# Row numbers of a group written behind its gates, and clearings tied to score tiles, in a one-core attention and mixture-of-experts kernel

## The chip, the core and the metric

The kernel runs on one core of one Trainium2 chip. The metric is the device time of one execution in microseconds. Two timed runs of the kernel before gave 2300.16 and 2305.29 us, median 2302.72 us. One more execution was profiled; it took 2296.34 us. Lines such as L443 are lines of the kernel before, unless the text says that they are of the changed kernel. PE is the matmul engine, DVE the vector engine, ACT the scalar engine, POOL the GpSimd engine, SP the engine that only issues transfers here.

## The reference

The inputs are u and v of shape 8 x 2496 x 256 and z of shape 8 x 2496 x 64, in float32, with an expert layer of 8 experts (256 to 1024 to 256).

```python
scores = (1 / S) * z @ z.T                    # per batch, S = 2496
out = (np.maximum(scores, 0) ** 2) @ v
x = (u * out).reshape(B * S, D)               # 19968 tokens of 256
logits = normalised(x) @ normalised(expert_emb).T / tau
expert_idx = argmax(logits, axis=1)           # one expert a token
gate = softmax(logits)[expert_idx]
out[token] = gate * (np.maximum(x @ w1[e], 0) @ w2[e])
```

The products are made from pairs of 16-bit halves (a value's rounded half and what is left of it), three products for one.

## The kernel before, in words

**Stage one, attention and routing.** The scores are symmetric, so a batch's 20 key tiles of 128 rows stand against five groups of up to 512 queries (the last has 448), and a score tile that lies above the diagonal is made once and reached again by a transposing DMA. There are 8 batches x 5 groups = 40 groups, and for each of them a loop over 20 key tiles. A step of this loop (the loop over `steps` at the end of the function) has three kinds of work:

- `scores` (L255 to L265): two matmuls into `sc`, then ACT makes relu and the square in `a`; three tiles ahead of their use.
- `parts` (L267 to L296): DVE splits `a` into two 16-bit halves, a cast (L284) and a subtraction (L285), in `hl` or in `joint`; `state["dv"]` is always the latest of these casts. SP issues the transposing DMA.
- `values` (L313 to L327): six matmuls of the halves with the halves of v, into two accumulators `acc` (L323, L325, L327).

PE follows the order of the program as it is written. DVE, ACT and POOL follow an order that a scheduler makes from the program by its own estimate of when things are ready; an engine then runs its list strictly in that order, and an instruction that waits holds up everything behind it. `tc.issue_after(ins)` adds an edge for this order alone: what is written under it comes behind `ins` on its own engine, without a semaphore.

**Routing.** When a group's 20 steps are over, `route` (L342 to L493) returns a list of pieces, and one of them runs behind the `values` of each later step. `gate_x` (L360) multiplies both accumulators with u into `xt`, which has one buffer (L362, two instructions). `turn` (L365) turns `xt` on PE (L368, L369), two steps later at the first; ACT copies the result and sums its squares (L379, L375). `root` (L618 to L632) and `scale` make scales on DVE, `splits` (L405, L406) write each token's x as two 16-bit halves into `row`, `top` and `exps` choose the expert, `gates` (L436 to L443) writes two more columns of `row`: the gate (L441) and the token's number (L443), `rank` and `place` find the row of the buffer `xs` that each token goes to (`dsti`, L467), and `scatters` issues four indirect DMAs from POOL, which carry `row` to `xs` (L473).

`row` has two buffers that the groups use in turn (`rows[par]`). What a group writes into its buffer may not overwrite what the scatter of the group before the last one still reads. The token numbers (L443) depend on nothing but this: they are made of the constant `idb` and the number of the group.

**Other work of stage one.** DVE also searches the next batch's z and v for their greatest values (L117, from loads `scan` with two buffers), splits z (L188, L189) and v (L233), and converts the experts' weights (L514 to L566). Of the last, short v tile half of the low part is cleared (L230); in a batch's last, short group the last 64 columns of `xt` are cleared (L349). POOL issues the plain loads of all this, in the same list as the scatters.

**Stage two, the experts.** From about 1445 us on, 8 experts' tokens are read from `xs` in tiles of 256 or 128, with matmuls at L881 to L883 and L905 to L907, and scattered to the output (L912).

Of the kernel before, what the change touches and what calls it, by code (L numbers as in the profile page):

```python
# [14 lines left out]
ALU = mybir.AluOpType  # L15
# [4 lines left out]
P = 128  # L20
# [11 lines left out]
def ceil_div(a, b):  # L32
    return -(-a // b)
# [11 lines left out]
def relu2_attention_then_moe(ctx, tc, zT, uT, v, emb, tau, w1, w2, ident, tri, iota_e, out):  # L45
    nc = tc.nc
    B, D, S = uT.shape
# [170 lines left out]
    def v_split(b, s):  # L218
        vt = vraw.pop((b, s))
        vv = vring.tile([P, 2 * D], F16, name="vv", tag="vv")  # L220
        k = scan[b, "cv"]
        if s == NST - 1:

            lo, hi = slice(0, DQ), slice(DQ, P)
            vh = wk.tile([P, D], F16, name="vh", tag="vh", bufs=1)
            nc.scalar.activation(vv[lo, 0:D], vt[lo], AF.Copy, scale=k[lo])
            nc.vector.tensor_copy(vv[lo, D:], vv[lo, 0:D])
            nc.scalar.activation(vh[hi], vt[hi], AF.Copy, scale=k[hi])
            nc.vector.scalar_tensor_tensor(vv[hi, 0:D], vt[hi], k[hi], vh[hi], op0=ALU.mult, op1=ALU.subtract)
            nc.vector.memset(vv[hi, D:], 0.0)  # L230
        else:
            nc.scalar.activation(vv[:, 0:D], vt, AF.Copy, scale=k)
            nc.vector.scalar_tensor_tensor(vv[:, D:], vt, k, vv[:, 0:D], op0=ALU.mult, op1=ALU.subtract)  # L233
        Vs[b, s] = vv

    state = {"pm": False}
# [105 lines left out]
    def route(b, g, acc, ut):  # L342

        t0, n = groups[g]
        nj = ceil_div(n, P)
        eps, oinv = scan[b, "out"]
        xt = rt.tile([P, 2, 512], F32, name="xt", tag="xt", bufs=1)
        if n < nj * P:
            nc.vector.memset(xt[:, :, n:nj * P], 0.0)  # L349
        x = rt.tile([P, 4, 2 * XH], F32, name="x", tag="x", bufs=1)  # L350
        xk = x.rearrange("p j (k c) -> p j k c", k=2)[:, :, :, 0:P]
        par = (b * NG + g) % 2
# [2 lines left out]
        row = rows[par]  # L355
        rowi = row.bitcast(I32)
        row16 = row.bitcast(F16)
        loc = {}
# [77 lines left out]
        def gates():  # L436
            sm = rt.tile([P, 4], F32, name="sm", tag="sm")
            nc.vector.tensor_reduce(sm[:, :nj], loc["ex"][:, :nj, :], axis=AX.X, op=ALU.add)
            nc.vector.tensor_scalar_add(sm[:, :nj], sm[:, :nj], 1e-9)
            nc.vector.reciprocal(sm[:, :nj], sm[:, :nj])  # L440
            nc.vector.scalar_tensor_tensor(row[:, :nj, D:D + 1], sm[:, :nj].unsqueeze(2), oinv,  # L441
                                           loc["dn"][:, :nj].unsqueeze(2), op0=ALU.mult, op1=ALU.mult)
            nc.vector.tensor_scalar_add(rowi[:, :nj, D + 1:D + 2], idb[:, :nj].unsqueeze(2), float(b * S + t0))  # L443

        def rank():
            ob = loc["ob"].rearrange("p j e -> p (j e)")
# [44 lines left out]
        def sq(j):  # L491
# [3 lines left out]
        return [gate_x, lambda: None, turn(0), both(turn(1), take(0)), both(take(1), sq(0)), both(turn(2), sq(1)),  # L495
                both(turn(3), take(2)), both(take(3), sq(2)), sq(3), root, scale, top, exps, splits(0),
                splits(2), gates, rank, place, scatters]


# [472 lines left out]
    for i, (b, g, q, s) in enumerate(steps):  # L972
# [16 lines left out]
        if i == 6:  # L989
# [7 lines left out]
            idb = iot[:, 4 * E:4 * E + 4]  # L997
# [23 lines left out]
        if b == 0 and g == 0:  # L1021
            v_split(b, s)
        if b + 1 < B:
            if (g == NG - 2 and q >= NST - early) or (NG > 1 and g == NG - 1) or NG == 1:
                k = q - (NST - early) if g == NG - 2 else q + early
                if k < NST:
                    v_split(b + 1, k)
                    if k + VAHEAD < NST:
                        v_load(b + 1, k + VAHEAD)
            if g == max(0, NG - 2) and q == 0:  # L1030
                for k in range(min(VAHEAD, NST)):
                    v_load(b + 1, k)
            while todo and todo[0][0] <= i - b * NB and not (todo[0][1] and state["pm"]):
                with tc.issue_after(state["at"]), tc.issue_after(state["dv"]):
                    todo.pop(0)[2]()
# [11 lines left out]
        if q == NST - 1:  # L1047
            while queue:
                queue.pop(0)()
            queue = route(b, g, accs.pop((b, g)), uts.pop((b, g)))  # L1050
            if b == B - 2 and g == NG - 1 and KA:
                queue.append(table_a)
            queue.pop(0)()
# [100 lines left out]
```

## Time and profile before

| what | value |
|---|---|
| timed runs, median | 2302.72 us (2300.16 to 2305.29) |
| profiled execution, own time | 2296.34 us |
| its span, first to last instruction | 2294.6 us |
| mean granted PE clock over the span | 0.984 |
| PE busy | 2166.9 us, 94% |
| DVE busy | 1373.0 us, 60% |
| ACT busy | 1062.1 us, 46% |
| POOL busy | 538.4 us, 23% |

How to read it: "busy" is an engine's time inside instructions. A matmul's end is modelled, so that 512 columns show 0.38 us while the next one starts 0.216 us later. A row of a table of waits gives the waiting engine and line, what it waited for, the total in us, the number of waits and the longest. In a timeline, what stands in brackets is the engine's idle time ahead of the instruction and what ended it. In a table by windows each row has a stretch of the span, its length, each engine's busy time with the number of its instructions, the granted PE clock, the mean busy share of the DMA engines, and GB/s.

### The profile page before, as it was taken

The page shows a single profiled execution, that of the slowest core. Times are in us where ns is not written, and L with a number is a line of the kernel's source. Part 1 is how long each engine was busy: PE and PEld are TensorE (multiplying, and loading weights), DVE is VectorE, ACT ScalarE, POOL GpSimd, SP SyncE. Part 2 cuts the span into 40 slices and gives each one's busy share as a digit, 9 for nine tenths or more (in the row PEclk, how much of TensorE's full clock was granted, in tenths as well). Part 3 has the DMA queues.
Part 4 walks back from the last instruction along what each step waited for, and adds up shares of the span by engine and source line. Part 5 has one row for each costly group of instructions (what it writes and reads, how often), then busy time and mean ns, then how long its engine had stood idle before and what let it go on. Part 6 is the DMA issues. An engine that isn't in the chain of part 4 may idle for free. (4 is left out here: it accounts for less than half of the span.)

```text
span 2294.6 us, 41344 instructions
## 1 busy us (share of the span) xinstructions
PE 2166.9 (94%) x14634; PEld 1416.5 (62%) x14634; DVE 1373.0 (60%) x4067; ACT 1062.1 (46%) x2193; POOL 538.4 (23%) x695
## 2 busy tenths in 40 slices
PE   6898999989999989999899999999999999999999
PEld 2444444444444444444444444788888888888898
DVE  7777767767778777687777855633333333333333
ACT  7566557656756656566666654222222222222221
POOL 1214124133134124224213201121212121212121
PEclk9999999999999999999999999999999999999999
DMA  7847766783974975776665573442333333237675
GB/s 190 197 98 194 149 161 164 142 211 99 173 195 116 203 152 146 162 163 183 133 153 132 118 166 78 126 119 66 75 84 75 84 93 66 50 82 205 141 194 129
DMA packets 518035, 313.84 MB, mean 137 GB/s; under 512 B 473845, under 2 KB 479230, under 8 KB 509632
## 3 DMA queue, kind: packets, MB, share of 16 engines
q1 hardware_dynamic: 474400, 165.55, 36.7%
q0 software_dynamic: 43136, 145.22, 21.0%
q8 instruction: 117, 1.92, 0.4%
q14 instruction: 94, 0.77, 0.1%
q10 hardware_dynamic: 288, 0.39, 0.1%
HBM read 277.53 MB, written 59.60 MB: 147 GB/s over the span
## 5 line engine op out<-in xcount | busy, mean ns | idle before, releaser
L263 ACT ACTIVATE a<-sc 128x512 f32<-128x512 f32 (+1 forms) x480 | 269.7, 562 | 193.1 <-PE sc L261 119.9
L912 POOL DMA_INDIRECT out_dram<-ot,me x159 | 154.6, 972 | 675.4 <-DVE ot L911 643.2
L264 ACT ACTIVATE a<-a 128x512 f32<-128x512 f32 (+1 forms) x480 | 286.8, 598 | 13.1
L473 POOL DMA_INDIRECT xs<-row,dsti x160 | 169.3, 1058 | 470.9 <-DVE joint L284 169.0
L327 PEld LDWEIGHTS <-vv 128*128 128x128 f16 x1600 | 158.3, 99 | 189.2 <-issue 14.8
L325 PEld LDWEIGHTS <-vv 128*128 128x128 f16 x1520 | 150.3, 99 | 185.7 <-issue 37.0
L323 PEld LDWEIGHTS <-vv 128*128 128x128 f16 x1600 | 158.0, 99 | 164.5 <-issue 7.6
L907 PE MATMUL po<-w,hl 128*128 128x256 f16 x928 | 253.0, 273 | 0.0
L906 PE MATMUL po<-w,hh 128*128 128x256 f16 x928 | 253.0, 273 | 0.0
L905 PE MATMUL po<-w,hh 128*128 128x256 f16 x928 | 253.0, 273 | 0.0
L323 PE MATMUL acc<-tt,vv 128*128 128x512 f16 (+1 forms) x640 | 242.2, 378 | 0.0
L325 PE MATMUL acc<-tt,vv 128*128 128x512 f16 (+1 forms) x640 | 242.0, 378 | 0.0
L911 DVE TENSOR_SCALAR ot<-po,me,w 128x256 f32<-128x256 f32 x116 | 58.3, 541 | 220.3 <-PE po L907 220.3
L327 PE MATMUL acc<-tt,vv 128*128 128x512 f16 (+1 forms) x640 | 188.7, 377 | 0.0
L260 PE MATMUL sc<-z 128*128 128x512 f16 (+1 forms) x480 | 176.4, 367 | 5.9 <-DVE z L189 3.1
L261 PE MATMUL sc<-z,z 128*128 128x512 f16 (+1 forms) x480 | 176.3, 367 | 0.0
L379 ACT COPY x<-pt 128x264 f32<-128x264 f32 x160 | 59.7, 373 | 172.4 <-PE pt L369 170.0
L906 PEld LDWEIGHTS <-hh 128*128 128x128 f16 x1272 | 124.4, 98 | 15.3 <-issue 1.0
L907 PEld LDWEIGHTS <-hl 128*128 128x128 f16 x1272 | 124.4, 98 | 14.4
L905 PEld LDWEIGHTS <-hh 128*128 128x128 f16 x1272 | 124.4, 98 | 14.2
L368 PE MATMUL pt<-rhs,xt 128*128 128x136 f32 x320 | 69.2, 299 | 44.2 <-DVE xt L362 43.0
L368 PEld LDWEIGHTS pt<-rhs,xt 128*128 128x128 f32 x320 | 60.8, 200 | 77.2 <-DVE xt L362 54.3
(3890 smaller groups left out, 5266.5 us busy)
## 6 DMA issues: line engine op xcount, KB each, us to landing
w<-wsd SPq DMA_DIRECT2D x64, 1026.0 KB
wa<-wsd SPq DMA_DIRECT2D x46, 1024.0 KB
w<-wsd SPq DMA_DIRECT2D x42, 1024.0 KB
wb<-wsd SPq DMA_DIRECT2D x24, 1026.0 KB
vt<-in_v_dram POOLq DMA_DIRECT2D x140, 128.0 KB, 2.8
scan<-in_v_dram POOLq DMA_DIRECT2D x56, 320.0 KB, 4.1
wr<-in_w_dram POOLq DMA_DIRECT2D x16, 1024.0 KB, 7.1
wsd<-wo POOLq DMA_DIRECT2D x16, 1024.0 KB, 5.2
```

The lines of the kernel that those rows point to most:

```text
L260: nc.tensor.matmul(sc[:, :n], z1[:, ss], z1[:, t0:t0 + n], start=True, stop=False)
L261: nc.tensor.matmul(sc[:, :n], z1[:, ss], z2[:, t0:t0 + n], start=False, stop=True)
L263: state["at"] = nc.scalar.activation(a[:, :n], sc[:, :n], AF.Relu, scale=2.0 ** -SHIFT).ins
L264: nc.scalar.activation(a[:, :n], a[:, :n], AF.Square)
L323: nc.tensor.matmul(o, va, ph, start=first, stop=False)
L325: nc.tensor.matmul(o, vb, ph, start=False, stop=False)
L327: nc.tensor.matmul(o, vb if last else va, pl, start=False, stop=ends)
L473: put = nc.gpsimd.indirect_dma_start(xs[:, :], bass.IndirectOffsetOnAxis(ap=loc["dsti"][:m, j:j + 1], axis=0), row[:m, j, :], None)
L905: nc.tensor.matmul(o, hh[:, f, t], wh, start=(f == 0), stop=False)
L906: nc.tensor.matmul(o, hh[:, f, t], wl, start=False, stop=False)
L907: nc.tensor.matmul(o, hl[:, f, t], wh, start=False, stop=(f == NF - 1))
L912: put = nc.gpsimd.indirect_dma_start(out, bass.IndirectOffsetOnAxis(ap=me.bitcast(U32)[:, j, 1:2], axis=0), ot[:, j, :], None, bounds_chec ...
```

## The change

Three instructions of DVE are tied to a place in the order. The token numbers come behind the gates of the same group. Both clearings come behind the score tile's cast that was the latest when they were written in the program. Nothing is added, left out or changed in size.

```diff
@@ v_split, the last key tile
             nc.vector.scalar_tensor_tensor(vv[hi, 0:D], vt[hi], k[hi], vh[hi], op0=ALU.mult, op1=ALU.subtract)
-            nc.vector.memset(vv[hi, D:], 0.0)
+            with tc.issue_after(state["dv"]):
+                nc.vector.memset(vv[hi, D:], 0.0)
@@ route
         if n < nj * P:
-            nc.vector.memset(xt[:, :, n:nj * P], 0.0)
+            with tc.issue_after(state["dv"]):
+                nc.vector.memset(xt[:, :, n:nj * P], 0.0)
@@ route, gates
-            nc.vector.scalar_tensor_tensor(row[:, :nj, D:D + 1], sm[:, :nj].unsqueeze(2), oinv,
-                                           loc["dn"][:, :nj].unsqueeze(2), op0=ALU.mult, op1=ALU.mult)
-            nc.vector.tensor_scalar_add(rowi[:, :nj, D + 1:D + 2], idb[:, :nj].unsqueeze(2), float(b * S + t0))
+            gw = nc.vector.scalar_tensor_tensor(row[:, :nj, D:D + 1], sm[:, :nj].unsqueeze(2), oinv,
+                                                loc["dn"][:, :nj].unsqueeze(2), op0=ALU.mult, op1=ALU.mult).ins
+            with tc.issue_after(gw):
+                nc.vector.tensor_scalar_add(rowi[:, :nj, D + 1:D + 2], idb[:, :nj].unsqueeze(2), float(b * S + t0))
```

The added lines shift the numbers: the cast L284 is L285 in the changed kernel, the subtraction L285 is L286, `xt` L362 is L364, the gate L441 is L443, and the token numbers L443 are L446.

The lists of PE, ACT and SP are the same in both kernels. On POOL, at two places (one in the second batch, one in the sixth), the load of u and one of three scan loads change places. On DVE the rows move as follows.

Before, DVE at the end of the second batch's first group: `hl` and `joint` are halves of score tiles, `mx` the search in an expert's weights, `xt` the product that PE turns, `row_99` the buffer of the group after it.

```order
L284 CAST hl__2747<-a 128x4x128
L285 TENSOR_TENSOR hl__2747<-a,hl__2747 128x4x128
L443 TENSOR_SCALAR row_99<-iot 128x4
L284 CAST hl__2769<-a 128x4x128
L514 TENSOR_REDUCE mx<-wr_2473 128x1
L285 TENSOR_TENSOR hl__2769<-a,hl__2769 128x4x128
L514 TENSOR_REDUCE mx<-wr_2473 128x1
L362 TENSOR_TENSOR xt<-acc_2341,ut 128x512
```

The same place in the changed kernel:

```order
L285 CAST hl__2747<-a 128x4x128
L286 TENSOR_TENSOR hl__2747<-a,hl__2747 128x4x128
L285 CAST hl__2769<-a 128x4x128
L517 TENSOR_REDUCE mx<-wr_2473 128x1
L286 TENSOR_TENSOR hl__2769<-a,hl__2769 128x4x128
L517 TENSOR_REDUCE mx<-wr_2473 128x1
L364 TENSOR_TENSOR xt<-acc_2341,ut 128x512
```

The token numbers are gone from this place; those of each group now stand next to its gate, or one row behind it.

Before, DVE at the seam of the first two batches, some rows behind the routing of the first batch's fourth group: `dsti` are the scatter's rows, `wo` converted weights.

```order
L467 TENSOR_REDUCE dsti<-pos 128x4
L284 CAST hl__2289<-a 128x448
L566 SCALAR_TENSOR_TENSOR wo<-wr_825,wup,wo 128x512
L285 TENSOR_TENSOR hl__2289<-a,hl__2289 128x448
L566 SCALAR_TENSOR_TENSOR wo<-wr_825,wup,wo 128x512
L284 CAST hl__2310<-a 128x4x128
L285 TENSOR_TENSOR hl__2310<-a,hl__2310 128x4x128
L443 TENSOR_SCALAR row_100<-iot 128x4
L284 CAST hl__2331<-a 128x4x128
```

The same place in the changed kernel:

```order
L470 TENSOR_REDUCE dsti<-pos 128x4
L285 CAST hl__2289<-a 128x448
L569 SCALAR_TENSOR_TENSOR wo<-wr_825,wup,wo 128x512
L286 TENSOR_TENSOR hl__2289<-a,hl__2289 128x448
L569 SCALAR_TENSOR_TENSOR wo<-wr_825,wup,wo 128x512
L285 CAST hl__2310<-a 128x4x128
L351 MEMSET xt 128x2x64
L286 TENSOR_TENSOR hl__2310<-a,hl__2310 128x4x128
L285 CAST hl__2331<-a 128x4x128
```

The token numbers are gone and the clearing of `xt`, which stood some rows earlier before, has come in.

A third place, at the end of the second group of the second batch and again of the sixth: before, DVE, with `wm`, `wmb` and `dg` from the scales of the weights and `smxv` the search in v.

```order
L285 TENSOR_TENSOR hl__3203<-a,hl__3203 128x4x128
L527 TENSOR_SCALAR wmb<-wm 2x1
L362 TENSOR_TENSOR xt<-acc_2773,ut 128x512
L529 TENSOR_SCALAR dg<-idt,wmb 2x2
L362 TENSOR_TENSOR xt<-acc_2774,ut 128x512
L117 TENSOR_REDUCE smxv<-scan 128x1 x2
```

In the changed kernel:

```order
L530 TENSOR_SCALAR wmb<-wm 2x1
L117 TENSOR_REDUCE smxv<-scan 128x1
L532 TENSOR_SCALAR dg<-idt,wmb 2x2
L364 TENSOR_TENSOR xt<-acc_2773,ut 128x512
L364 TENSOR_TENSOR xt<-acc_2774,ut 128x512
L286 TENSOR_TENSOR hl__3203<-a,hl__3203 128x4x128
L117 TENSOR_REDUCE smxv<-scan 128x1
```

One of the two searches now stands ahead of both products, and the subtraction behind them.

## The prediction

> **What bounds the kernel now.** I read the table by windows first, to see which stage the change can touch.
>
> ```profile
> core 0: us, PE busy (x) PEld busy (x) DVE busy (x) ACT busy (x) POOL busy (x), PEclk, DMA share, GB/s
> 100.00:1430.00 1330.00, 1232.95 (x6118) 616.29 (x6117) 973.07 (x3217) 796.85 (x1717) 358.19 (x495) 0.98 0.66 153
> 1445.00:2295.00 850.00, 842.09 (x8093) 756.67 (x8090) 315.86 (x592) 194.48 (x333) 162.69 (x167) 1.00 0.43 107
> ```
>
> Stage two is PE, 842 of 850 us at full clock, and the change moves nothing in it. In stage one PE is the fullest engine too, but it stands still for 97 of 1330 us and its clock is not full; DVE is busy for 973 us, 73%. So stage one ends when PE does, and I look for what holds PE. The table of DVE's waits has as its largest rows of stage one:
>
> ```profile
> DVE row L443 <- DMA xs<-row,dsti: 99.3, 24, 5.5
> DVE xn2c L618 <- ACT sq L375: 59.5, 15, 8.7
> DVE smxv L117 <- DMA scan<-in_v_dram: 42.9, 20, 5.3
> ```
>
> The first row is the token numbers: 24 of the 40 wait for the scatter that last read their buffer, 99.3 us, 4.1 us each. DVE is not the fullest engine, so this costs only what PE then lacks. PE's table of waits, the rows that matter here:
>
> ```profile
> PE pt L368 <- DVE xt L362: 43.0, 17, 5.5
> PE pm L449 <- DVE ob L427: 15.6, 6, 3.6
> PE pm L141 <- DVE wm L524: 4.4, 2, 2.6
> PE acc L323 <- DVE hl__10565 L284: 2.7, 1, 2.7
> PE acc L323 <- DVE hl__14653 L284: 0.6, 1, 0.6
> ```
>
> The timeline ties the two. This is one of the 24 places: POOL's last scatter of a group, DVE, then PE.
>
> ```profile
> 245.44 0.90 POOL L473 DMA_INDIRECT xs<-row,dsti  x1 [0.30 <-issue]
> ...
> 243.37 0.69 DVE L285 TENSOR_TENSOR hl__2747<-a,hl__2747 128x512 f16<-128x512 f32 x1
> 248.01 0.17 DVE L443 TENSOR_SCALAR row<-iot 128x4 int32<-128x4 f32 x1 [3.95 <-DMA xs<-row,dsti]
> 248.11 0.43 DVE L284 CAST hl__2769<-a 128x512 f16<-128x512 f32 x1
> ...
> 250.24 1.28 DVE L362 TENSOR_TENSOR xt<-acc,ut 128x512 f32<-128x512 f32 x2
> ...
> 245.25 0.59 PE L327 MATMUL acc<-joint,vv 128*128 128x512 f16 x2
> ...
> 247.84 0.59 PE L327 MATMUL acc<-tt,vv 128*128 128x512 f16 x2
> ```
>
> DVE is free at 244.06, stands for 3.95 us until a scatter has landed, and everything behind the token numbers starts late: a cast, a subtraction, two searches in a weight, and the product `xt`. PE ends the group's accumulators at 245.84, has 2.6 us of other work ahead of the turn (to 248.43) and then waits:
>
> ```profile
> 250.98 0.50 PE L368 MATMUL pt<-rhs,xt 128*128 128x136 f32 x2 [2.54 <-DVE xt L362]
> ```
>
> I went through the 24 places like this, one by one: each is followed within 4 us by a wait of PE. The first and the last, DVE and PE:
>
> ```profile
> 142.34 0.17 DVE L443 TENSOR_SCALAR row<-iot 128x4 int32<-128x4 f32 x1 [3.88 <-DMA xs<-row,dsti]
> 143.10 0.27 PE L141 MATMUL pm<-smbv,ones_f 1*128 1x1 f32 x1 [2.59 <-DVE wm L524]
> ...
> 1425.40 0.17 DVE L443 TENSOR_SCALAR row<-iot 128x4 int32<-128x4 f32 x1 [3.22 <-DMA xs<-row,dsti]
> 1427.06 0.38 PE L368 MATMUL pt<-rhs,xt 128*128 128x136 f32 x1 [1.25 <-DVE xt L362]
> ```
>
> In 15 places PE waits for `xt`, in 7 for a cast (`hl`, at the seams of batches), in 2 for `wm`.
>
> **The change part by part.** *Token numbers behind the gates.* The instruction itself, 0.17 us, is neither added nor taken away; its wait goes. By then the buffer must be free anyway, because the row splits of the same group stand ahead of the gates and write it first; the wait for the scatter falls to them. The smallest room over all groups is the last one's: its token numbers were let go at 1425.40 (above), its first split runs here:
>
> ```profile
> 1463.16 0.35 DVE L405 TENSOR_SCALAR row<-x,up 128x256 f16<-128x256 f32 x1
> ```
>
> That is 38 us after the landing, so the moved wait finds its scatter done. I price it at nothing.
>
> What PE gets back, by the rows above. Of the 43.0 us for `xt`, two waits belong to a late scan load, not to the token numbers:
>
> ```profile
> 106.59 0.82 DVE L117 TENSOR_REDUCE smxv<-scan 128x1 f32<-128x640 f32 x1 [5.35 <-DMA scan<-in_v_dram]
> 108.07 0.59 PE L368 MATMUL pt<-rhs,xt 128*128 128x136 f32 x1 [5.48 <-DVE xt L362]
> ...
> 822.91 0.82 DVE L117 TENSOR_REDUCE smxv<-scan 128x1 f32<-128x640 f32 x1 [2.56 <-DMA scan<-in_v_dram]
> 824.39 0.38 PE L368 MATMUL pt<-rhs,xt 128*128 128x136 f32 x1 [4.48 <-DVE xt L362]
> ```
>
> So `xt` gives 43.0 - 5.5 - 4.5 = 33.0 us in 15 waits. The seven casts run from 2.7 us (`hl__10565`) to 0.6 us (`hl__14653`), 12.9 us together. `wm` gives 4.4 us. Sum: 50.3 us. That is half of DVE's 99.3 us; the other half was PE's cushion, as in the place shown, where DVE would have come to `xt` (2.1 us behind the token numbers) at about 246.2 us, just behind the accumulators, and with 1.3 us for the two products the turn would have found them at 247.5 us.
>
> *The clock.* Right after the place shown the windows say:
>
> ```profile
> 251.60:255.00 3.40, 3.40 (x10) 1.86 (x11) 2.14 (x4) 0.89 (x3) 0.75 (x1) 0.50 0.49 139
> ...
> 1360.90:1364.30 3.40, 3.40 (x11) 1.86 (x11) 0.76 (x2) 0.89 (x3) 0.75 (x1) 0.50 0.71 146
> ```
>
> For 3.4 us the granted clock is 0.50 and PE gets 10 or 11 matmuls done; with a full clock it is 19:
>
> ```profile
> 255.00:258.40 3.40, 3.40 (x19) 1.00 0.47 93
> ```
>
> Eleven of the 24 places are followed by such a stretch (these are the first and the last); each costs half of 3.4 us, 1.7 us, together 18.7 us. If the wait of PE brings them on, they go with it. The Trainium skill ("TensorE: Matmul & The Clock Gate", section "HAM oscillation — how this bites in real kernels") gives the rule as no idle gaps of PE over some 3.4 us; by it, waits of 0.6 to 3.2 us would not lower the clock and this term would be nothing. The trace speaks against the rule as a threshold: the half clock begins 0.6 us behind a gap of 2.54 us.
>
> *Clearings.* 16 instructions of 0.165 us, now inside a cast and subtraction:
>
> ```profile
> L349 DVE MEMSET xt<- x8: 165/165/165, 187.3 to 1434.2; 128x128 f32 x8
> L230 DVE MEMSET vv<- x8: 165/165/165, 60.4 to 1273.1; 64x128 uint32 x8
> ```
>
> 2.6 us at most over the kernel, on an engine with 27% idle time: nothing. Without that cover it would be the 2.6 us.
>
> *The search ahead of `xt`.* At two places one search in v now stands ahead of the products. The second of these before:
>
> ```profile
> 1003.07 0.67 DVE L362 TENSOR_TENSOR xt<-acc,ut 128x512 f32<-128x512 f32 x1
> ...
> 1003.80 0.67 DVE L362 TENSOR_TENSOR xt<-acc,ut 128x512 f32<-128x512 f32 x1
> 1004.68 0.82 DVE L117 TENSOR_REDUCE smxv<-scan 128x1 f32<-128x640 f32 x1 [0.21 <-DMA scan<-in_v_dram]
> ```
>
> It waited until 1004.68 for its load; ahead of `xt` (there at 1003.07) it would take 0.8 us and wait up to 1.7 us. PE had no wait at these two turns, so some of it is absorbed: between 0 and 2 x 2.5 us, with two clock stretches 8.4 us. I take 2, nearer the lower end.
>
> *What comes back.* With the token numbers gone something else is last. The 25 turns that had no such wait show how much: 10.0 us for late scan loads, 0.4 us each. For the 15 freed turns that makes 6 us, and I add 1 us, some half of a stretch at half clock: 7 us back. The lower bound is nothing, the upper one half of the sum (below). A faster stage one raises the DMA share only from 0.66 to about 0.69, so I add nothing for contention.
>
> **Sum:** 50.3 + 18.7 - 2 - 7 = 60 us off the profiled execution's own 2296.3 us, 2236.3 us. That execution lies 6.4 us under the median of the timed runs, 2302.72 us; I add half of this and predict **2239 us**.
>
> **The rivals.**
>
> *Another wait takes the place.* Scan loads and the squares of ACT also hold DVE (42.9 and 59.5 us), and the six waits for `ob` (15.6 us, at each seam, where DVE itself is late) stay. If these take half of the 69 us back, the time is 2296.3 - 34.5 + 3 = 2265 us. For it: the scan chain has two buffers, and two of the 25 free turns show it. Against it: 23 of 25 do not.
>
> *The clock does not follow.* If the stretches at half clock have other causes, 18.7 us stay: 2258 us. For it: the mean of 0.98 over 1330 us is 27 us, some 16 stretches, so five have no token numbers ahead of them, and 13 of the 24 waits have no stretch behind. Against it: eleven stand right behind a wait. It is what the Trainium skill's rule above would give.
>
> *The wait was hidden.* If PE's waits for `xt` were due to the accumulators being late and not to DVE's list, nothing moves: 2299 us. Against it: the accumulators of the place shown were done 4 us ahead of `xt`.
>
> *Slower.* The wait for the scatter moves to the row splits. If scatters land later than those start, all 38 groups with a predecessor wait there, on the path that leads to the gates, at 4.1 us each and PE's half of it: 38 x 4.1 x 0.51 = 79 us, and 38 x 11 / 24 x 1.7 = 30 us of clock, against 69 us saved: 2296.3 + 40 + 3 = 2339 us. It decides from the point at which scatters slip by 38 us or more. Against it: they have landed 2.6 us after the last issue in the place shown.
>
> **How the numbers follow.** Forecast 0.72, another wait 0.14, the clock 0.06, hidden 0.05, slower 0.03. The range goes down to 2216 us (all 69 us and 11 of the 15.6 us for `ob`, should DVE reach the seams earlier) and up to 2272 us, past the first two rivals; what lies beyond is hidden, slower, and tails. A measurement of this kernel tells about 2% from no change, that is 2256.7 us here. Faster by more: nearly all of the forecast and small parts of two rivals, 0.77. Within 2%: the rest of those and hidden, 0.20. Slower: 0.03.
>
> **What would show it.** Right: the row of DVE waiting for `xs<-row,dsti` is gone and no such wait stands at the splits; PE's wait for `xt` falls from 43 us to some 16; the seven waits for casts at the seams are gone; stretches at half clock in stage one fall from 16 to five or six; stage two keeps its 850 us. Wrong: a wait for scatters at the splits, DVE's idle time come back as waits for `scan`, or a full set of half-clock stretches without the waits.

## The result, and the profile after

The changed kernel took 2222.5 us (median of 2219.11 and 2225.89), against 2302.72 us before: a ratio of 0.9652, with a 95% interval of 0.957 to 0.973. Timed again with seven executions of the changed kernel and eleven of the kernel before, the ratio was 0.9637, interval 0.961 to 0.966 (the last run below). The forecast was 2239 us in a range of 2216 to 2272 us: the right way, inside the range, the gain 80 us where 64 were forecast.

The profiled execution took 2219.11 us, its span 2217.2 us. First the table by windows, with the two stages cut where they now lie:

```profile
100.00:1353.00 1253.00, 1208.85 (x6118) 609.74 (x6117) 973.91 (x3215) 795.66 (x1717) 359.73 (x494) 0.99 0.70 162
1368.00:2217.00 849.00, 841.60 (x8088) 756.40 (x8083) 316.15 (x594) 194.10 (x333) 162.82 (x167) 1.00 0.43 107
```

The 6118 matmuls that took 1330 us of stage one before take 1253 us; stage two is as long as it was. In the table of DVE's waits neither the token numbers nor the splits wait for `xs<-row,dsti` any more (one wait of `xt`, 0.4 us, is put down to it); its largest rows of stage one are those that stood second and third before:

```profile
DVE xn2c L621 <- ACT sq L377: 68.4, 18, 8.4
DVE smxv L117 <- DMA scan<-in_v_dram: 40.3, 15, 5.4
```

PE's waits, the rows that answer to those shown of before:

```profile
PE pm L452 <- DVE ob L429: 15.5, 6, 3.7
PE pt L370 <- DVE xt L364: 10.7, 3, 5.4
```

The wait for `xt` fell from 43.0 us in 17 to 10.7 us in 3, the two behind late scan loads and a small one. The seven waits for casts and the two for `wm` that the prediction counted are gone; other casts still hold PE, for up to 2.2 us each. The place that the prediction took as its example, DVE and PE:

```profile
235.00 0.69 DVE L286 TENSOR_TENSOR hl__2747<-a,hl__2747 128x512 f16<-128x512 f32 x1
235.77 0.43 DVE L285 CAST hl__2769<-a 128x512 f16<-128x512 f32 x1
...
237.91 1.28 DVE L364 TENSOR_TENSOR xt<-acc,ut 128x512 f32<-128x512 f32 x2
...
239.46 0.59 PE L328 MATMUL acc<-tt,vv 128*128 128x512 f16 x2
239.89 0.40 PE L370 MATMUL pt<-rhs,xt 128*128 128x136 f32 x2
240.12 0.40 PE L371 MATMUL pt<-rhs,xt 128*128 128x136 f32 x2
```

Between the subtraction and the next cast DVE now stands for 0.08 us instead of 4 us, and PE goes from `values` to the turn without a bracket. The token numbers wait for nothing where they are now, and neither does the first split, to which the wait for the scatter fell; the views of these two lines name no idle time ahead of them:

```profile
L446 DVE TENSOR_SCALAR row<-iot x40: 161/165/168, 93.1 to 1392.7; 128x4 int32<-128x4 f32 x40
```

```profile
L407 DVE TENSOR_SCALAR row<-x,up x160: 310/348/523, 77.8 to 1388.8; 128x256 f16<-128x256 f32 x160
```

**Where the 77 us came from.** PE issues the same 14,634 matmuls in the same order in both kernels, so the two traces can be laid over each other, matmul by matmul, and the difference of each step from one start to the next sorted: PE's waits of over 0.15 us, what else differs in steps that touch a stretch at half clock, and the rest. The other two columns do the same with the profiled executions of two runs below: the token numbers tied alone, and the changed kernel once more.

| us saved against the profiled execution of before | changed kernel | token numbers alone | changed kernel, once more |
|---|---|---|---|
| waits of PE over 0.15 us | 50.7 | 49.4 | 42.7 |
| steps that touch a stretch at half clock | 16.4 | 14.9 | 5.2 |
| the rest (in the first column nearly all inside the turns, L368 and L369) | 10.1 | 9.2 | 11.5 |
| sum, from the first matmul to the last | 77.2 | 73.5 | 59.4 |

The last column is the slowest of the seven executions, 2236.6 us, and it shows how much the parts vary: two executions of one kernel differ by 8.0 us in waits elsewhere and 11.2 us at half clock. The 24 matmuls of PE that waited behind the token numbers don't vary: they waited for 50.5 us before and for none in all three columns.

### The profile page after: what moved, and what is told of

Its sections match the earlier page's. It is cut to its first block, busy times and chain, and to the rows that moved or that the text cites. A ratio compares the mean times of both kernels' runs of the same rounds, so it can differ in the third digit from the quotient of the medians.

```text
span 2217.2 us, 41314 instructions
## 1 busy us (share of the span) xinstructions
PE 2141.7 (97%) x14634; PEld 1409.6 (64%) x14634; DVE 1374.8 (62%) x4067; ACT 1060.1 (48%) x2193; POOL 540.5 (24%) x695
## 4 chain that ended last, share of the span: by engine, by line
PE 70%; DVE 10%; DMA 7%; issue 6%; ACT 4%; POOL 3%; SPq 0%; POOLq 0%; DVEq 0%; ACTq 0%
PE acc L328 9%; PE acc L324 9%; PE acc L326 8%; PE po L908 6%; PE po L910 6%; PE po L909 6%; PE sc L261 3%; PE sc L262 3%; POOL xs L476 2%; DMA wsd<-wo 2%; DMA scan<-in_v_dram 1%; PE pt L371 1%; PE pt L370 1%; ACT a L265 1%; ACT a L264 1%
## 5 line engine op out<-in xcount | busy, mean ns | idle before, releaser
L324 PE MATMUL acc<-tt,vv 128*128 128x512 f16 (+1 forms) x640 | 236.9, 370 | 0.0
L326 PE MATMUL acc<-tt,vv 128*128 128x512 f16 (+1 forms) x640 | 236.8, 370 | 0.0
L328 PE MATMUL acc<-tt,vv 128*128 128x512 f16 (+1 forms) x640 | 184.3, 370 | 0.0
L195 POOL DMA_DIRECT2D vt<-in_v_dram x140 | 76.2, 546 | 82.4 <-DVE vv L234 40.2
L908 PE MATMUL po<-wb,hh 128*128 128x256 f16 x344 | 93.8, 273 | 1.0 <-DMA wb<-wsd 1.0
```

The lines of the kernel that those rows point to most:

```text
L324: nc.tensor.matmul(o, va, ph, start=first, stop=False)
L326: nc.tensor.matmul(o, vb, ph, start=False, stop=False)
L328: nc.tensor.matmul(o, vb if last else va, pl, start=False, stop=ends)
L908: nc.tensor.matmul(o, hh[:, f, t], wh, start=(f == 0), stop=False)
```

## The experiments

Times are medians; each ratio is against the kernel before, run beside it on the same chip (its medians there were 2297 to 2310 us).

**Which part of the change.** The first run ties the token numbers alone (`...` stands for lines left out):

```diff
             nc.vector.memset(vv[hi, D:], 0.0)
...
             nc.vector.memset(xt[:, :, n:nj * P], 0.0)
...
+            with tc.issue_after(gw):
+                nc.vector.tensor_scalar_add(rowi[:, :nj, D + 1:D + 2], idb[:, :nj].unsqueeze(2), float(b * S + t0))
```

> The token numbers are tied behind their gates, both clearings stay where the kernel before has them. Theory (the wait of the token numbers is all): about 2223 us, the changed kernel's time within 0.5%, no wait of DVE for scatters, PE's wait for xt some 11 us. Rival (the clearings inside score tiles, or the reordering as a whole, give part of it): over 2240 us.

Measured: 2219.3 us, ratio 0.961 (0.9575 to 0.964); PE's wait for `xt` 10.8 us in 3. The second ties the clearings alone:

```diff
+            with tc.issue_after(state["dv"]):
+                nc.vector.memset(vv[hi, D:], 0.0)
...
+            with tc.issue_after(state["dv"]):
+                nc.vector.memset(xt[:, :, n:nj * P], 0.0)
...
             nc.vector.tensor_scalar_add(rowi[:, :nj, D + 1:D + 2], idb[:, :nj].unsqueeze(2), float(b * S + t0))
```

> Both clearings are tied, the token numbers stay untied. Theory: 2303 us within 0.5%, DVE still waits some 99 us for scatters in 24 places. Rival (the clearings give part of it): under 2285 us.

Measured: 2307.3 us, ratio 0.9985 (0.997 to 1.000), with DVE's wait as in the kernel before:

```profile
DVE row L445 <- DMA xs<-row,dsti: 99.8, 24, 6.3
```

The token numbers are the whole of it; the clearings are worth nothing that can be measured.

**The dose.** Token numbers of every other group:

```diff
-            nc.vector.tensor_scalar_add(rowi[:, :nj, D + 1:D + 2], idb[:, :nj].unsqueeze(2), float(b * S + t0))
+            with (tc.issue_after(gw) if par else nullcontext()):
+                nc.vector.tensor_scalar_add(rowi[:, :nj, D + 1:D + 2], idb[:, :nj].unsqueeze(2), float(b * S + t0))
```

> Only the token numbers of every other group (the 20 groups with the second row buffer) are tied; the clearings stay as before. Of the 24 places 13 are in these groups, with 27.1 of the 50.5 us of PE's waits and 6 of the 11 stretches at half clock. Theory (each place is paid by itself): about 0.54 of the gain, 2260 us, between 2250 and 2270; 11 waits of DVE for scatters are left, some 45 us. Rival (a place removed is paid at the next one, DVE or PE catch up): under a quarter of the gain, over 2283 us. Rival (one kind of place carries it all): near 2223 or near 2303 us.

Measured: 2264.2 us, ratio 0.9795 (0.976 to 0.983), 46 us below the 2310.0 us of the kernel before beside it, where the full change's ratio makes 84 us: 0.55 of it (by the ratio's interval, 0.46 to 0.67). DVE's and PE's waits:

```profile
DVE row L444 <- DMA xs<-row,dsti: 46.5, 11, 5.5
...
PE pt L368 <- DVE xt L362: 28.4, 11, 5.7
```

13 of the 24 waits went, and with them the share of the gain that their own PE waits had foretold (0.54). Of the 50.5 us at the 24 matmuls of PE, 24.9 us are left. So these places are paid one by one, and what is saved at one is not lost at the next.

**The wait without the token numbers.** The changed kernel, with an instruction added that has the same wait, since it writes into the same buffer, and whose numbers nothing uses:

```diff
             with tc.issue_after(gw):
                 nc.vector.tensor_scalar_add(rowi[:, :nj, D + 1:D + 2], idb[:, :nj].unsqueeze(2), float(b * S + t0))
+            nc.vector.tensor_scalar_add(rowi[:, :nj, D + 2:D + 3], idb[:, :nj].unsqueeze(2), float(b * S + t0))
```

> The changed kernel, with one more instruction for each group that writes the same numbers into a column of the row buffer that nothing reads, and is not tied. It brings the wait for the scatter back without moving the token numbers or the clearings; it adds 40 x 0.17 us to DVE. Theory (the wait in the middle of DVE's list is the cost): about 2303 us, 24 waits, some 99 us, half-clock stretches back to some 16. Rival (the token numbers next to their gates, or the order of the other rows, make the gain): 2223 to 2230 us.

Measured: 2303.0 us, ratio 0.998 (0.996 to 1.000): the whole gain is lost again.

```profile
DVE row L447 <- DMA xs<-row,dsti: 99.1, 24, 6.6
...
PE pt L370 <- DVE xt L364: 44.9, 18, 6.1
```

At 22 of the same 24 matmuls PE waits again, for 49.1 us where it was 50.5. The token numbers themselves are where the change puts them, as are the clearings. So it is not their nearness to the gates that helps, but that nothing in the middle of DVE's list waits for a scatter.

**Would another buffer have done?** To make room for a third row buffer, both runs have a shorter ring for v; the first is the control.

```diff
-    vring = actx.enter_context(tc.tile_pool(name="vring", bufs=NST + 5))
+    vring = actx.enter_context(tc.tile_pool(name="vring", bufs=NST + 1))
```

> The kernel before with a ring of 21 instead of 25 buffers for the halves of v, only to make room for the next run, its control. No theory rests on its time; expected 2300 to 2320 us with the same 24 waits for scatters.

The second, against the control:

```diff
-    rows = [cst.tile([P, 4, ROW], F32, name=f"row{i}") for i in range(2)]
+    rows = [cst.tile([P, 4, ROW], F32, name=f"row{i}") for i in range(3)]
...
-        row = rows[par]
+        row = rows[(b * NG + g) % 3]
```

> The control, with three row buffers instead of two and the token numbers untied. Theory (the scheduler lists an instruction that waits for nothing but a buffer at the moment at which it takes the buffer to be free, whichever buffer that is, and that moment is too early on the chip): the token numbers stand at the same places of DVE's list, one group further ahead, and the 24 waits, some 97 us, and the time of the control stay within 0.7%. Rival (two buffers are too few): the waits go and the time falls by about 75 us under the control's.

Measured: control 2315.7 us, ratio 1.009 (1.006 to 1.012); three buffers 2313.7 us, ratio 1.007 (1.004 to 1.009), 0.1% apart. The waits, control and then three buffers:

```profile
DVE row L443 <- DMA xs<-row,dsti: 83.7, 24, 6.1
```

```profile
DVE row L443 <- DMA xs<-row,dsti: 76.0, 22, 6.4
```

A third buffer does not cure it: the scheduler lists the token numbers a group earlier, at the same places. In the control's trace a group's token numbers stand behind the scatters of the group two before; with three buffers they stand behind those of the group three before, the one that frees their buffer, and as many products `xt` stand ahead of them as, in the control, ahead of those of the group before. The cause is the place in the list, not the shortage of buffers.

**Three more waits of the same kind.** On the changed kernel, the scales tied like the token numbers; the ranking matmuls two steps later; the second half of the scans four steps later; and all three.

```diff
 def root():
-            loc["s"], loc["n2c"] = sqrt_of(n2[:, :nj], (P, nj), "x")
+            with tc.issue_after(state["dv"]):
+                loc["s"], loc["n2c"] = sqrt_of(n2[:, :nj], (P, nj), "x")
```

> The changed kernel, with the first scales of a group (the square root's chain on DVE) tied behind the cast that is the latest when they are written. In the changed kernel DVE waits 68 us there for ACT's squares, and at two places (about 455 and 1134 us) PE then waits, 7.0 us together, each with a stretch at half clock. Theory (a waiting instruction at the head of DVE's list costs PE what is queued behind it, and the clock follows): those four waits of PE go, about 2210 us. Rival (the scales come later and with them the choice of experts, which PE waits for at the seams): PE's 15.5 us for ob grow, 2222 us or more.

Measured: 2216.5 us, ratio 0.963 (0.9605 to 0.965). Beside the changed kernel's 2222.5 and 0.9637 that is 2 to 6 us, not 12; the intervals overlap, so that any gain at all is not shown. The theory failed: the four waits fell from 7.0 to 5.8 us only. Two casts hold PE for 1.1 us each instead of 2.2, but a score wait there grew from 1.8 to 2.6 us. PE's wait for `xt` fell to 2.2 us besides, and PE now waits in two other places for a scale (3.5 us), so that its waits are as long in sum as the changed kernel's.

```diff
-                splits(2), gates, rank, place, scatters]
+                splits(2), gates, lambda: None, lambda: None, rank, place, scatters]
```

> The changed kernel, with PE's ranking matmuls (which wait for ob, 15.5 us at six seams, up to 3.7 us) two steps later in the program. Theory: PE has 2.6 us of other work in that time, so most of the 15.5 us and two stretches at half clock go: about 2203 us, between 2198 and 2212. Rival (DVE is what is late at the seams, and PE then waits there for casts or for xt instead): 2218 us or more.

Measured: 2209.4 us (2209.1 to 2216.0), ratio 0.9604 (0.958 to 0.963), inside the range of the theory. The wait that was 15.5 us in six:

```profile
PE pm L452 <- DVE ob L429: 1.5, 3, 0.7
```

```diff
-            todo.append((at + 2 * i, False, lambda w=what: scan_load(b + 1, *w)))
-            todo.append((at + 2 * i + 4, False, lambda w=what: scan_max(b + 1, *w)))
+            c = at + 2 * i + (4 if i >= 5 else 0)
+            todo.append((c, False, lambda w=what: scan_load(b + 1, *w)))
+            todo.append((c + 4, False, lambda w=what: scan_max(b + 1, *w)))
...
-        at += 2 * len(SCANS) + 4
+        at += 2 * len(SCANS) + 8
```

> The changed kernel, with the second half of the scan loads and searches of a batch four steps later, so that fewer stand ahead of xt just when POOL is busy with scatters. In the changed kernel PE waits 10.7 us in three places for xt behind a late scan load, with three units of half clock. Theory: these go, about 2208 us. Rival (the loads are as late at the later place): 2220 us.

Measured: 2243.5 us, ratio 0.974 (0.972 to 0.976). Both theory and rival were wrong: it is slower than the changed kernel by some 20 to 24 us. The waits aimed at did go, but others grew:

```profile
PE pm L452 <- DVE ob L429: 26.8, 7, 4.7
PE pm L131 <- DVE smz L129: 17.6, 6, 7.0
...
PE pt L370 <- DVE xt L364: 1.1, 2, 0.6
```

PE's waits are 83 us in sum, where the two executions of the changed kernel have 69 and 77 us. A likely reading, which no run tests, is that the later scans push the scales of the next batch (`smz`) towards the seam, where DVE is late already.

> The three edits before together, on the changed kernel. Theory (each place is paid by itself): the sum of the three gains, 2177 us, between 2165 and 2195. Rival (they meet in the same stretches, at the seams where DVE is full): no better than the best of the three.

Measured: 2241.1 us, ratio 0.975 (0.970 to 0.980). The three do not add up, and with the scan shift among them the time is that of the scan shift alone. The last of these, without it:

> The changed kernel with two of the three further edits, the scales tied behind the latest cast and the ranking matmuls two steps later. They gave 2216.5 and 2209.4 us alone. Theory (each place is paid by itself): some 5 and 12 us under the changed kernel's 2221, 2204 us, between 2199 and 2209. Rival (they meet at the seams): no better than 2209 us.

Measured: 2223.0 us (2215.1 to 2228.1), ratio 0.969 (0.966 to 0.971): the rival's side, and by the ratio, whose interval lies above both of theirs, worse than either edit alone. The profiled execution has a new wait:

```profile
PE acc L324 <- DVE hl__7491 L285: 4.5, 1, 4.5
```

That execution was the fastest of the four, 2215.1 us, and its waits are as long in sum as the changed kernel's (69.0 and 68.9 us). So why the other three took 2221 to 2228 us stays open.

**The changed kernel in more rounds.**

> The changed kernel as it is, timed in more rounds beside the kernel before, since its ratio has a wide interval from two runs each (0.957 to 0.973). Theory: the ratio lies at 0.962 to 0.967, that is 2216 to 2227 us where the kernel before has 2303. If the ranking two steps later is worth 12 us, its ratio of 0.9604 stays below this one; if not, this one comes down to it.

Measured: 2224.0 us (2221.4 to 2236.6), ratio 0.9637 (0.961 to 0.966). The ranking two steps later, 0.9604 (0.958 to 0.963), is likely better by some 8 to 13 us, its four times all lie below these seven; but the two were not timed side by side and the intervals overlap, so this is not shown.

## Why the prediction was right, and where its sizes were off

- *PE is what the token numbers cost.* Right, and shown from three sides: the part alone, half of the dose, and the wait brought back by another instruction. Price 50.3 us by the table of waits; at the 24 places 50.5 us went, all there was.
- *What comes back, 7 us.* This term failed. Outside the 24 places PE's waits of over 0.15 us in stage one, from 28 us on, were 46.3 us before and 46.0 us after. I had taken the 25 undisturbed turns as a sample of what the 15 others would meet, but their 10 us were two late scan loads, which came at the same two turns again (10.2 us). In the second execution of the changed kernel, waits outside the 24 places were 8 us longer than in the first; that they were not longer in the first is in part luck.
- *The clock, 18.7 us.* Right in kind, and its size in part luck: 16.4 us in the profiled execution, 5.2 us in the second. Of stage one's 16 stretches seven were left, and ten in the second execution, where five or six were forecast; two were of double length before, two after, and four in the second execution.
- *The search ahead of `xt`, 2 us.* It cost 0.6 us, at one of the two places:

```profile
952.46 0.82 DVE L117 TENSOR_REDUCE smxv<-scan 128x1 f32<-128x640 f32 x1 [1.91 <-DMA scan<-in_v_dram]
...
954.06 0.38 PE L370 MATMUL pt<-rhs,xt 128*128 128x136 f32 x1 [0.56 <-DVE xt L364]
```

- *Left out: the second half of the turn.* 10.1 us were saved in steps that no table of PE's waits shows, nearly all in the turns, 4.4 us of them between L368 and L369. When `xt` is late, PE waits for its first half, and then again for a short time for the second, which DVE finishes 0.6 us later: after the wait at 682.90 us L369 starts 0.60 us behind L368, in the undisturbed turn shown above 0.23 us. That the other 5.7 us have the same cause is likely, but not shown apart. The wait stood in the profile of before, in the view of L369, and is nearly gone after, in that of L371; kernel before, then changed kernel:

```profile
  DVE xt L362: 7.2, 25
```

```profile
  DVE xt L364: 0.9, 3
```

- *The moved wait at the splits, priced at nothing; the clearings, nothing.* Both right.
- *The rivals.* "Another wait takes the place", "hidden" and "slower" did not come. "The clock does not follow" is refuted by the runs as a whole: time at half clock over the span was 75.5 us before, 92.6 us with the clearings alone and 85.6 us with the wait brought back; it was 44.0 and 53.0 us in the two executions after, 35.6 us with the token numbers alone tied, and 68.3 us with half of them.

So the forecast of 60 us was short of the profiled execution's 77 us by the 7 us of return and the 10 us in the turns, less some 2 us of clock. One bound is uneven: the 2216 us leave out the 3 us that the other sums add for the profiled execution; with them it is 2219 us, still under the 2222.5 us measured.

## What to carry to other kernels

An instruction that depends on almost nothing is one that a scheduler can put in a bad place: here it was listed as soon as its buffer was thought to be free, and when it was not free then, everything behind it on that engine stood still. Look in the waits for a trivial instruction that waits for a transfer, price it by the waits of the busiest engine that follow each of its waits and not by its own total (50 of 99 us here), count the lost clock and the short second waits with it, and tie it behind work that needs the same buffer later anyway. A further buffer did not help. Do not count on such edits to add up: of the next three, one is likely worth 8 to 13 us alone, one 2 to 6 us at most, one cost some 20 us, and together they gave less than the best of them.

## What the runs showed of the hardware

The half clock follows a rule that is sharper than a limit on one gap. Its changes lie on a fixed grid of 3.41 us: in each trace all but the last, at the end of the program, lie within 1 ns of a grid of 3.4133 us. In all 14 traces PE's idle time (gaps over 0.1 us) was summed in each interval of that grid that ran at full clock, from 95 us to the first matmul of stage two, and the clock of the next interval noted:

| idle in the interval, us (nearest 0.2) | next at full clock | next at half clock |
|---|---|---|
| 0.0 to 1.2 | 4919 | 0 |
| 1.4 | 35 | 1 |
| 1.6 | 24 | 4 |
| 1.8 | 30 | 9 |
| 2.0 | 12 | 17 |
| 2.2 to 3.4 | 0 | 130 |

So about half an interval of idle time decides, whether in one gap or in several. In the kernel before, the example's gap of 2.54 us fell into one interval, and the next was at half clock:

```profile
248.19:251.60 3.41, 0.77 (x5) 0.32 (x3) 3.41 (x7) 0.00 (x0) 0.00 (x0) 1.00 0.18 38
251.60:255.01 3.41, 3.41 (x10) 1.87 (x11) 2.14 (x4) 0.89 (x3) 0.75 (x1) 0.50 0.50 141
```

A longer one of 3.20 us, which ended at 198.57, was cut by the grid into 1.6 and 1.6 us and cost no clock:

```profile
193.57:196.98 3.41, 1.79 (x10) 0.81 (x9) 3.41 (x17) 1.45 (x4) 3.01 (x6) 1.00 0.74 218
196.98:200.39 3.41, 1.82 (x14) 1.00 (x14) 3.30 (x17) 2.58 (x6) 1.69 (x4) 1.00 0.51 150
200.39:203.80 3.41, 3.41 (x19) 1.69 (x18) 3.34 (x8) 2.49 (x5) 2.80 (x3) 1.00 0.41 116
```

This fits the 24 waits of the kernel before: seven left 2.1 us or more of idle time in one interval, and all seven were followed by half clock; of the 17 others, with at most 1.9 us in one interval, four were. The grid lies differently in each execution (its changes come 2.42 us behind a multiple of 3.4133 us from the first instruction in the kernel before, and 1.11 and 2.71 us in the two executions of the changed kernel), so which waits are cut by it changes too. The page "TensorE: Matmul & The Clock Gate" of the Trainium skill (section "What's actually happening") has the window of 3.41 us and that it is not aligned with the kernel; both agree with the grid here. Its rule of no idle gap over some 3.4 us (section "HAM oscillation — how this bites in real kernels") does not: 2.2 us in one interval was enough each time.
